# Retention attention and a gated MLP on one core: a new fixed order for all five engine queues

## The chip, the cores and the metric

The kernel runs on one core of one Trainium2 chip. The metric is device time in microseconds (us), from the start of an execution to its end; a result is the median of several runs. The kernel before takes 211.69 us, the median of 3 runs that lie between 211.59 and 213.75 us.

A core has five engines with a queue of instructions each, worked off in order: TensorE (PE, matmuls and transposes), VectorE (DVE), ScalarE (ACT), GpSimd (POOL) and SyncE (SP), which here issues the DMA transfers of the main work. An engine waits with all that stands behind an instruction until the data of that instruction are there. So the order in which instructions are put into each queue is itself a part of the kernel, and it is the part that changes here.

## The reference

```python
# q, k, v: (8 batches, 8 heads, 576, 64)
scores = (1 / sqrt(64)) * q @ k^T                  # per batch and head
D[i, j] = gamma[h] ** (i - j) if i >= j else 0
x = (scores * D) @ v                               # no softmax
x = x.transpose(0, 2, 1, 3).reshape(8, 576, 512)
h = gelu_tanh(x @ w_in)                            # w_in: 512 x 1024
u, v = h[..., :512], h[..., 512:]
v_n = layernorm(v) * g_ln                          # over the 512
v_s = einsum('ts,bsd->btd', w_sg, v_n) + b_sg      # w_sg: 576 x 576, mixes positions
out = x + (u * v_s) @ w_out                        # w_out: 512 x 512, float32 out
```

The attention has no softmax, only a decay with the distance. So it can be done in chunks: inside a chunk the masked scores, and from one chunk to the next a running sum of k^T v per head (called Z here). The second half is a gated MLP whose gate mixes the 576 positions of a batch through `w_sg`.

## The kernel before

**Tiling.** The 8 batches go in 4 pairs (p = 0 to 3). A pair has 1152 rows, 9 tiles of 128; tile 4 lies half in one batch and half in the other. For the attention each pair is cut into 5 units (two tiles, two tiles, the middle tile, two tiles, two tiles), so there are 20 units, 0 to 19; units 2, 7, 12 and 17 are the middle ones, of half the width. Tiles are numbered 0 to 35 through all pairs.

**The jobs.** The program is built as 925 jobs, numbered in the order in which `add` is called. A job is a few instructions on one engine. Those that the text speaks of, with the lines of their instructions in the kernel before:

- loads on SP, 512 KB each in most cases (`a_load`, L457 and L460; the middle units take the L460 line, two transfers of 128 KB), `load(b,q)`, `load(b,k)` and `load(b,v)` of unit b. For most units one load of q of 1 MB serves two units.
- casts to bfloat16, with the decay factors multiplied in for q and v (`a_prep`: L493 k, L503 q and v), on POOL; unit 0 has its q on DVE and its k on ACT (L491).
- `T`: transposes of q and k on PE (`a_T`, L540), taken to SBUF by DVE (L555). From unit 10 on, all but the middle units have theirs transposed by DMA instead (`a_TX`, L560).
- `S`: scores (`a_S`, L591), masked on DVE (L604). `Z`: the running sum (`a_Z`, L627), added up on DVE and cast on ACT. `O` and `O2`: the attention's output in two parts (`a_O`, `a_O2`, L673), brought to x by ACT (L730).
- `V` (`m_V`, L741) and `U` (`m_U`, L788): x times the two halves of w_in. After V come gelu on ACT (L748), statistics on DVE (L756, L757), the rs group, one over the standard deviation, on POOL (L761 to L764), and the norm on ACT (L773 for the middle tile, L776 for others). After U comes gelu on ACT (L798).
- `W`: the spatial mixing of a batch (`m_W`, L807), multiplied with u on DVE (L817). It needs the norms of all five tiles of its batch and the transposed spatial weight.
- `m_O(i)`: the output of tile i (L838). For the first pair x is added by further matmuls (L833) and the result evacuated on ACT (L853); later pairs have x transposed back by a DMA (`m_X`, L847) and added on DVE (L855). Then a store on SP (`m_store`, L860).

**The start.** The weights come in through the same SP queue: the second half of w_in (for V), w_sg in three pieces (two large ones of 576 KB and a small one), the first half of w_in (for U) and w_out. ACT and DVE cast w_in (L388, L390), ACT casts w_sg (L413). Then ten jobs on PE transpose the spatial weight (`build_wT`, L921), each with an evacuation on DVE. `to_col`, `to_rows`, `place_vmid` and `place_wT` (L909 to L914) put g_ln and b_sg into additional rows of the operands of W. `fill(n)` (L357) puts matmuls on zeros into PE's queue, whose result nobody reads, n units of 128 columns.

**What sets the order.** A string `ORDER` lists all job numbers, and a name such as `f10` for `fill(10)`. In the kernel before, `plan` calls `follow`: it takes from `ORDER` only the order within each engine, estimates each job's start with a small cost model (semaphores, DMA rings, blocks of instructions, changes of kind on PE), and `emit` writes the jobs in the order of these estimated starts. Per engine this is again the order of `ORDER`. The order between engines does matter for which buffers are shared: a tile pool hands its buffers out in rotation, in the order of the calls. The numbers of buffers are fixed in `BUFS`: 8 for loads (`ld`), 2 for the large q (`ldq`), 2 each for the casts of q and k and for the transposed q and k, 2 PSUM buffers for T, S and O (`pp`), 4 for everything else in PSUM (`d`), 3 for V's gelu (`vg`), 4 for the output (`ob`), 5 for x transposed back (`xr`).

## Time and profile before

| | |
|---|---|
| median of 3 runs (lowest to highest) | 211.69 us (211.59 to 213.75) |
| profiled execution, span from first to last instruction | 211.8 us |
| PE busy (matmuls) | 193.5 us, 91% |
| PE's weight loads, beside the matmuls | 134.4 us, 63% |
| DVE busy | 146.7 us, 69% |
| ACT busy | 116.3 us, 55% |
| POOL busy | 117.9 us, 56% |
| HBM read and written | 32.79 MB and 9.44 MB, 199 GB/s |

The span is the time between the first and the last instruction of one profiled execution, and it is within 0.1 us of the median. A busy share is the share of that span. In the lists of waits and of the chain, an arrow `<-` names what ended the wait: a job on another engine by its line, a DMA by its tensors, or "issue", where nothing that the profile shows was waited for. In names such as `qb<-ld,gpow` the output stands on the left and the inputs on the right.

### The profile page before, as it was taken

What the parts mean: (1) busy time and instruction counts of PE and PEld (TensorE: products, weight loads), DVE (VectorE), ACT (ScalarE), POOL (GpSimd) and SP (SyncE); (2) the same over time, 40 slices, a digit from 0 to 9 for tenths busy, and PEclk for the clock granted to TensorE, in tenths of its full rate; (3) what the DMA queues carried; (4) which work ended last, traced back from release to release, by engine and by line L of the source; (5) the groups of instructions that cost most, each with busy time, mean ns of one, the idle gap of its engine ahead of it and who ended that gap; (6) DMA issues with size and microseconds to landing.
All of it is one profiled execution on the core that took longest, in us unless ns stands there. A gap on an engine that the chain in (4) does not pass through costs nothing.

```text
span 211.8 us, 7654 instructions
## 1 busy us (share of the span) xinstructions
PE 193.5 (91%) x3257; PEld 134.4 (63%) x3288; DVE 146.7 (69%) x287; ACT 116.3 (55%) x207; POOL 117.9 (56%) x169
## 2 busy tenths in 40 slices
PE   7995598799999999989999979989989999999992
PEld 6873366576677666757676657656647676565660
DVE  4585487978767688648767647778676757977483
ACT  5233656993696753784775745617544574363400
POOL 8738375897599699920849598044349440322000
PEclk9999889999999999999999999999999999999999
DMA  5999899999799999999898989999789986936685
GB/s 157 334 274 323 140 377 273 259 347 320 146 316 319 317 208 289 181 258 326 245 253 110 219 155 345 237 129 248 197 217 264 254 193 187 225 115 149 176 249 198
DMA packets 94228, 50.45 MB, mean 238 GB/s; under 512 B 45354, under 2 KB 87602, under 8 KB 94194
## 3 DMA queue, kind: packets, MB, share of 16 engines
q1 hardware_dynamic: 94176, 49.97, 96.9%
q8 instruction: 25, 0.41, 0.9%
q14 instruction: 9, 0.07, 0.2%
q10 hardware_dynamic: 18, 0.00, 0.0%
HBM read 32.79 MB, written 9.44 MB: 199 GB/s over the span
## 4 chain that ended last, share of the span: by engine, by line
PE 62%; DMA 16%; SPq 5%; POOL 5%; DVE 3%; ACT 3%; issue 3%; POOLq 0%; ACTq 0%
PE wp L807 15%; PE op L838 11%; PE hu L788 11%; PE hv L741 11%; PE pp L673 5%; DMA xT<-in_moe_w_sg_dram 4%; DMA xT<-in_moe_w_in_dram 4%; PE pp L591 3%; DMA ld<-in_k_dram 3%; DMA kT<-kb 3%; SPq L560 3%; DMA ld<-in_q_dram 2%; PE zp L627 2%; SPq L457 2%; POOL vb L503 2%
## 5 line engine op out<-in xcount | busy, mean ns | idle before, releaser
L604 DVE TENSOR_TENSOR ret<-pp,msk 128x1024 bf16<-128x1024 f32 x32 | 38.7, 1216 | 6.4 <-PE pp L591 6.4
L503 POOL TENSOR_TENSOR vb<-ld,gpow 128x1024 bf16<-128x1024 f32 (+1 forms) x20 | 34.6, 1731 | 14.7 <-DMA ld<-in_v_dram 9.1
L807 PE MATMUL wp<-wT,vn 128*128 128x288 bf16 x256 | 40.8, 286 | 0.0
L788 PE MATMUL hu<-xT,w_in 128*128 128x256 bf16 (+1 forms) x320 | 36.7, 262 | 0.2 <-ACT zb L659 0.2
L741 PE MATMUL hv<-w_in,xT 128*128 128x512 bf16 x125 | 35.1, 380 | 1.4 <-issue 0.3
L817 DVE TENSOR_TENSOR uT<-wp,uT 128x288 bf16<-128x288 f32 x64 | 27.9, 449 | 11.5 <-PE wp L807 11.0
L838 PE MATMUL op<-w_out,uT 128*128 128x512 bf16 (+1 forms) x136 | 34.3, 373 | 0.6
L730 ACT ACTIVATE xT<-pp 128x512 bf16<-128x512 f32 (+1 forms) x40 | 20.6, 552 | 25.8 <-PE pp L673 24.0
L788 PEld LDWEIGHTS <-w_in 128*128 128x128 bf16 x320 | 28.2, 98 | 7.0 <-issue 0.5
L756 DVE BATCH_NORM_STATS2 bst<-vg 128x6 f32<-128x512 f32 x36 | 24.7, 687 | 10.1 <-ACT vg L748 10.0
L776 ACT ACTIVATE vn<-vg,mv 128x512 bf16<-128x512 f32 x32 | 25.3, 807 | 11.1 <-POOL mv L764 11.0
L748 ACT ACTIVATE vg<-hv 128x512 f32<-128x512 f32 x36 | 21.3, 594 | 17.0 <-PE hv L741 13.3
L807 PEld LDWEIGHTS <-vn 128*128 128x128 bf16 x256 | 24.2, 98 | 8.4 <-issue 0.2
L761 POOL TENSOR_SCALAR mv<-mv 128x2 f32<-128x2 f32 (+1 forms) x20 | 4.5, 224 | 42.2 <-DVE mv L757 38.3
L503 POOL TENSOR_TENSOR qb<-ldq,gpow 128x1024 bf16<-128x1024 f32 x14 | 26.5, 1902 | 0.9 <-DMA ldq<-in_q_dram 0.8
L798 ACT ACTIVATE uT<-hu 128x512 bf16<-128x512 f32 x36 | 20.9, 595 | 7.9 <-PE hu L788 7.9
L855 DVE TENSOR_TENSOR ob<-op,xr 128x512 f32<-128x512 f32 (+1 forms) x28 | 18.4, 668 | 6.1 <-PE op L838 5.8
L838 PEld LDWEIGHTS <-uT 128*128 128x128 bf16 x148 | 13.7, 98 | 11.5
L741 PEld LDWEIGHTS <-xT 128*128 128x128 bf16 x144 | 13.2, 98 | 11.6 <-ACT xT L730 0.2
L807 PE MATMUL wp<-wT,vmid 128*128 128x288 bf16 x64 | 18.3, 287 | 0.0
L493 POOL CAST kb<-ld 128x1024 bf16<-128x1024 f32 x14 | 14.4, 1038 | 4.3 <-DMA ld<-in_k_dram 4.2
L762 POOL TENSOR_TENSOR mv<-mv,mhalf 128x2 f32<-128x2 f32 (+1 forms) x20 | 13.7, 686 | 1.7
(100 smaller groups left out, 248.9 us busy)
## 6 DMA issues: line engine op xcount, KB each, us to landing
out_dram<-ob SPq DMA_DIRECT2D x35, 256.0 KB, 3.5
ld<-in_k_dram SPq DMA_DIRECT2D x16, 512.0 KB, 6.9
ld<-in_v_dram SPq DMA_DIRECT2D x16, 512.0 KB, 6.7
ldq<-in_q_dram SPq DMA_DIRECT2D x7, 1024.0 KB, 8.4
xT<-in_moe_w_sg_dram SPq DMA_DIRECT2D x2, 576.0 KB, 9.0
ld<-in_q_dram SPq DMA_DIRECT2D x2, 512.0 KB, 6.3
xT<-in_moe_w_in_dram SPq DMA_DIRECT2D x1, 1024.0 KB
ld<-in_q_dram SPq DMA_DIRECT2D x8, 128.0 KB, 5.9
```

The source lines that it names most:

```text
L503: ve.tensor_tensor(dst, src, g.unsqueeze(len(src.shape) - 1).to_broadcast(list(src.shape)), op=Alu.mult)
L604: ins = nc.vector.tensor_tensor(ret[:].rearrange("p r (k t) -> p (r k) t", k=2), sc[:].rearrange("p r (k t) -> p (r k) t", k=2), (msk2 if ...
L730: nc.scalar.activation(dst, src, Act.Copy)
L741: ins = nc.tensor.matmul(hv[:], xTs[p][:, m, kk, :], w_in[:, kk, F2:], start=(kk == 0), stop=(kk == KK - 1))
L748: unfence(nc.scalar.activation(vgs[i][:], cur.pop(("hv", i))[:], Act.Gelu_apprx_tanh), ("V", i))
L756: nc.vector.bn_stats(bst[:], vgs[i][:])
L776: nc.scalar.activation(vn[:], vg[:], Act.Identity, scale=mv[:, s, 2:3], bias=mv[:, s, 3:4])
L788: ins = nc.tensor.matmul(hu[:, n, :], w_in[:, kk, 128 * c:128 * c + 128], xTs[p][:, m:m + w, kk, :], start=(kk == 0), stop=(kk == KK - 1), ...
L798: unfence(nc.scalar.activation(uTs[p][:, c0:c1, 128 * m:128 * m + 128 * w], cur.pop(("hu", i, half))[:], Act.Gelu_apprx_tanh), ("U", i, half))
L807: ins = nc.tensor.matmul(ps[:], vns[t0 + j][e][:, 128 * c:128 * c + 128], wT[e][j][:, half * HS:(half + 1) * HS], start=(j == 0), stop=(j ...
L817: ins = nc.vector.tensor_tensor(uTs[p][:, c, col:col + HS], cur.pop(("wp", b, c, half))[:], uTs[p][:, c, col:col + HS], op=Alu.mult)
L838: ins = nc.tensor.matmul(op[:], uTs[p][:, c, r], w_out[:, c, cs], start=(p >= XP and c == 0), stop=(c == KK - 1), skip_group_check=True)
```

## The change

Jobs, buffers and their numbers stay. The string `ORDER` is replaced by another one, which orders the same 925 jobs anew on all five queues, and `plan` takes the jobs straight from it: they are emitted in the order of the string, engines mixed as they stand there. The cost model (`ready`, `place`, `follow`, the tables at the top) is taken out; `ins` of some jobs changes, which nothing reads any more. The filler has two entries, `f1` and `f5`, in place of eight, 6 units instead of 47.

```diff
-SEM = {"PE": 205.0, "DVE": 35.0, "ACT": 35.0, "POOL": 35.0}
-OVL = {"PE": 0.0, "DVE": 60.0, "ACT": 90.0, "POOL": 50.0, "SP": 0.0}
-FETCH = (5400.0, 5000.0)
...
 ORDER = (
-    '0 f1 1 f3 2 f3 f2 72 f10 3 73 17 f5 103 6 104 7 106 105 75 107 f9 8 76 5 195 267 197 268 f14 269 4 22 198 16 15 '
-    '108 196 12 13 272 109 79 273 14 74 111 274 276 275 110 112 277 270 199 80 20 201 278 289 23 279 202 19 21 9 290 '
...
+    '2 f1 0 1 7 74 6 105 f5 75 3 103 76 12 104 267 106 8 269 107 17 195 108 197 77 198 196 109 72 14 73 111 268 272 '
+    '112 5 13 273 274 78 199 4 79 275 15 201 276 16 202 110 23 9 277 81 278 113 24 270 200 279 114 115 80 280 22 '
...
     def plan(self):
-        if ORDER:
-            return self.follow(ORDER)
...
+        self.done = [self.fill(int(x[1:])) if x[0] == "f" else self.jobs[int(x)] for x in ORDER.split()]
 
     def emit(self):
+        seen = set()
         for j in self.done:
+            assert all(d in seen for d in j.deps)
+            seen.add(j)
             j.fn()
+        assert all(j in seen for j in self.jobs)
```

The start of SP's queue, in the words of the list above (win1 is the half of w_in for V, win0 that for U, sg the large pieces of the spatial weight, sg4 its small piece):

```
before: q0 k0 v0 win1 sg4 q1 k1 v1 sg  sg q2 k2 v2 q3 win0 k3 k4 v3 k6 v4 k5 ...
after:  v0 q0 k0 k1 q1 win1 q2 v1 sg4 v2 k2 sg sg q3 win0 k3 k4 v3 v5 v4 k5 ...
```

And somewhat later, from the 27th entry on (st is a store of an output tile):

```
before: ... k7 v7 v8 q8 k8 k10 st1 q10 k9 k11 v9 q12 k12 v10 st2 st3 v11 st0 ...
after:  ... v6 q8 k8 k9 st2 st1 v7 v8 q10 v10 k10 k11 v9 st0 st3 x9 q10T k10T st4 ...
```

On PE the first jobs are, without the filler (wT is a build, with batch parity and column block; U has tile, width and half; W has batch, block and half):

```
before: T(0) col S(0,0) Z(0) S(0,1) O(0) rows1 O2(0) T(1) V(0) S(1,0) S(1,1) Z(1) V(1) wT(0,2) wT(0,0)
        O(1) T(2) O2(1) wT(1,4) rows0 wT(1,0) S(2) V(2) O(2) wT(0,1) wT(0,3) wT(1,2) Z(2) O2(2) V(3) ...
after:  col Z(0) T(0) S(0,0) S(0,1) rows0 T(1) O(0) O2(0) S(1,0) rows1 S(1,1) V(0) V(1) Z(1) T(2) Z(2)
        S(2) O(1) O2(1) O(2) O2(2) wT(0,1) wT(0,4) wT(1,1) wT(1,0) wT(1,2) V(2) wT(0,0) wT(1,4) V(4) ...
```

## The prediction

> **What bounds the kernel now.** I read the busy totals and the slices of the page first, then a table of stages, and then who TensorE (PE) waited for.

> ```profile
> span 211.8 us, 7654 instructions
> ...
> PE 193.5 (91%) x3257; PEld 134.4 (63%) x3288; DVE 146.7 (69%) x287; ACT 116.3 (55%) x207; POOL 117.9 (56%) x169
> ...
> q8 instruction: 25, 0.41, 0.9%
> ```
> ```profile
> 0.00:46.00 46.00, 37.21 (x712) 28.71 (x716) 30.62 (x73) 26.19 (x44) 30.46 (x57) 0.96 1.00 272
> 46.00:205.00 159.00, 153.25 (x2536) 104.18 (x2556) 113.36 (x210) 90.08 (x164) 87.46 (x114) 1.00 0.99 229
> ```
> ```profile
> 0.00:16.00 16.00, 12.54 (x52) 10.47 (x52) 1.00 0.98 255
> ```

> The columns are the stretch, its length, busy time and count of PE, weight loads, DVE, ACT and POOL, then the granted clock, the DMA share and GB/s. The third fence is the same table for line L357 alone, the filler. The first W job, the spatial mixing, starts at 46 us. Before it PE does only 37.2 - 12.5 = 24.7 us of real work in 46; after it, it is busy 153.25 of 159 and idle 5.75. So there are two places to win or lose: how much real work is done by 46 us, and the idle time after it. The waits of PE after 46 us:

> ```profile
> PE pp L673 <- issue: 1.2, 2, 0.9
> PE pp L591 <- DMA kT<-kb: 1.0, 1, 1.0
> PE pp L540 <- POOL qb L493: 1.0, 1, 1.0
> ```

> Three kinds of wait hold 3.2 of the 5.75 us. No large stall waits to be removed: the change can lift these and can make others of the same kind.

> **The change, part by part.** No job, buffer or byte changes except the filler. The planner's code leaves the host's side; it costs the chip nothing either way. What is left is positions in five in-order queues.

> *The start.* These rows tell when each load was there, by the first work that uses it:

> ```profile
> 5.19 1.23 DVE L503 TENSOR_TENSOR qb<-ld,gpow 128x1024 bf16<-128x1024 f32 x1 [0.84 <-DMA ld<-in_q_dram]
> ...
> 6.94 1.06 ACT L491 ACTIVATE qb<-ld 128x1024 bf16<-128x1024 f32 x1 [1.51 <-DMA ld<-in_k_dram]
> ...
> 8.87 1.90 POOL L503 TENSOR_TENSOR vb<-ld,gpow 128x1024 bf16<-128x1024 f32 x1 [1.33 <-DMA ld<-in_v_dram]
> ...
> 12.14 1.06 ACT L390 ACTIVATE w_in<-xT 128x1024 bf16<-128x1024 f32 x1 [4.14 <-DMA xT<-in_moe_w_in_dram]
> ...
> 14.40 1.90 POOL L503 TENSOR_TENSOR qb<-ld,gpow 128x1024 bf16<-128x1024 f32 x1 [3.63 <-DMA ld<-in_q_dram]
> ...
> 23.22 1.83 ACT L413 ACTIVATE wnat<-xT 128x576 bf16<-128x576 f32 x3 [1.73 <-DMA xT<-in_moe_w_sg_dram]
> ...
> 26.42 1.05 POOL L503 TENSOR_TENSOR vb<-ld,gpow 128x512 bf16<-128x512 f32 x1 [0.49 <-DMA ld<-in_v_dram]
> ...
> 35.14 0.64 PE L540 MATMUL pp<-ident,qb 64*128 64x64 bf16 x32
> ...
> 37.99 1.04 POOL L493 CAST kb<-ld 128x1024 bf16<-128x1024 f32 x1 [0.65 <-DMA ld<-in_k_dram]
> ...
> 44.21 1.65 ACT L773 ACTIVATE vmid<-vg,mv 64x512 bf16<-64x512 f32 x2 [0.18 <-POOL mv L764]
> ...
> 46.01 0.66 PE L807 MATMUL wp<-wT,vn 128*128 128x288 bf16 x4
> ```

> A 512 KB load takes 1.8 us of the queue (5.19, 6.94, 8.87). In the new order v, q and k of unit 0 arrive at about 5.2, 6.9 and 8.8, so the first transposes, which wait for both casts, start near 10. k and q of unit 1 come next, near 10.3 and 11.9 instead of 14.4; the first half of w_in slips by two such loads, 12.1 to about 15.5. The q of unit 2, v of unit 1, the small piece of the spatial weight and v and k of unit 2 now also stand ahead of the spatial weight's two large pieces. The first fifteen transfers are the same set in both orders, so what follows them (k of units 3 and 4, there at 37.99) is as early as before; the spatial weight takes the place in which unit 2's v landed, 26.4 instead of 23.2. Its casts, which ended at 25.05, then end near 28.5, and the builds start there.

> What PE does meanwhile is gained: S, Z and O of units 1 and 2, four of which stood behind the builds, come first. Walking the list with durations of before, T of unit 3's q is reached near 37 (35.14 before, where two of the ten builds came after it; now one does). Then the k of units 3 and 4 decides: T of k cannot run before 37.99 + 1.04, and the new POOL order puts one rs group (1.4) ahead of these casts, so 40.4 at the earliest; its evacuation (1.2), S, an S that waits for the other's evacuation, and W near 44.4 to 45.7. ACT's `place_vmid` (2.5 us) no longer stands in front of the norms that end at 45.9. Against 46.0 that is 0.3 to 1.6 sooner, but the O of unit 3 comes after W now, so 0.7 us less work is done by then. I take **-0.2**, with -2 and +2 as ends: the sooner end is a W that waits for nothing but the 40.4, the later one the 3.2 us of the spatial weight with two thirds uncovered.

> *The filler.* 47 units become 6. They take 12.5 us in which PE waits for loads, so removing them saves nothing by itself. What they may cover is the clock:

> ```profile
> 21.00:25.00 4.00, 1.36 (x35) 0.64 (x35) 2.34 (x3) 2.27 (x5) 0.82 (x2) 0.99 0.84 130
> 25.00:28.40 3.40, 3.29 (x75) 2.67 (x75) 1.97 (x6) 1.14 (x4) 1.97 (x3) 0.50 0.92 277
> ```

> After 4 us with 1.36 busy, the granted clock is 0.50 for 3.4 us, which costs 1.7 us of PE's time in before as well. I count one such stretch in each kernel, at 0. [...]

> *Changes of kind on PE.* Jobs are of three kinds (wide matmuls, attention, transposes). A change costs about a tenth of a microsecond:

> ```profile
> 73.74 0.57 PE pp L540 x32
> ...
> 77.04 0.25 PE zp L627 x28
> ...
> 92.12 1.73 PE hv L741 x8
> 93.84 0.87 PE hu L788 x8
> 94.72 0.61 PE wp L807 x5
> ...
> 98.81 0.57 PE pp L591 x32
> 99.38 0.72 PE wp L807 x5
> ```

> The rows are a T, a Z, two V, a U, a W, two S and a W. The second W stands at such a change, the first does not: 0.11. From the first W on there are 67 changes instead of 70: **-0.3**. The others that go are in the start, where PE waits anyway.

> *Blocks of instructions.* 25 fetches bring 0.41 MB, 16.4 KB each, for 3257 + 3288 = 6545 recorded PE instructions: about 256 in a block. One wait shows what a short block does:

> ```profile
> 85.27 0.23 PE pp L591 x14
> ...
> 89.39 0.26 PE pp L591 x16
> 89.65 0.05 PE pp L673 x3
> 89.69 0.94 issue
> 90.63 0.30 PE pp L673 x5
> ```

> PE stops in the middle of one job, with nothing to wait for but its instructions. Counting matmul and load as two, the 256 before the stop began at the piece of 85.27 and held 4.4 us of work; with the 0.94 the block took 5.3. I take 5.3 us as the least time of a block. In the new order I count off the blocks, with the durations of before and 0.1 for each change. One example: W, S and T of units 7 and 8, U, V, O of unit 7, Z and half an S of unit 8 make 256 instructions and 0.61 + 0.28 + 0.57 + 0.87 + 0.87 + 0.2 (20 of the small matmuls) + 0.25 + 0.15 and five changes, 4.3 us at most. Four blocks after the first W fall short: 4.3, 4.9, 4.2 (with 0.15 for the narrow S in the example) and 4.6, so 1.0 + 0.4 + 1.1 + 0.7 = 3.2 us of waiting. Before paid 1.2 (the "issue" row above). **+2.0**; ends -1.2 (all hidden) and +3.

> *Loads behind stores.* In before, SP issues `load(7,v)` (job 40) ahead of the store of output tile 1 (job 345); now it stands behind the stores of tiles 2 and 1.

> ```profile
> 55.67 0.89 SPq L460 DMA_DIRECT2D ld<-in_v_dram  x1
> ```
> ```profile
> 60.07 0.60 ACT L853 ACTIVATE ob<-op 128x512 f32<-128x512 f32 x1 [0.44 <-PE op L838]
> ```
> ```profile
> 69.57 0.68 PE pp L673 x40
> ```
> ```profile
> 150.43 0.57 SPq L860 DMA_DIRECT2D out_dram<-ob  x1
> ```
> ```profile
> ld<-in_k_dram SPq DMA_DIRECT2D x8, 128.0 KB, 5.6
> ld<-in_v_dram SPq DMA_DIRECT2D x8, 128.0 KB, 4.2
> ```

> Before, this load left at 55.7, some 14 us ahead of Z of unit 7 (just after the 69.57 row). Now the chain begins with matmul `m_O(1)`: two evacuations of unit 5, a norm and its own evacuation on ACT (0.6 + 0.6 + 0.8 + 0.6, the 0.8 worked out from 1.65 for the middle tile's two, ending 2.6 after its start), a store's issue 0.6, two load issues 1.1 (as long as the store's), landing 4.2, POOL's half-width multiply 1.05 (the 26.42 row): 9.55 us. PE has 8.05 us of work between, plus changes 0.5 and a block's 0.4: 8.9. **+0.6**; all of PE's queue stands behind that Z. Ends: 0, and 3.6 with the landing of the k row (+1.4), both issues as slow as the 0.89 of the 55.67 row (+0.7) and ACT one evacuation and one norm later (+1.0). Behind it are the O of output tile 0 and a U, none of which can pass.

> The DMA-transposed units, where 1.0 was waited (kT), lie as far behind their POOL casts in PE's work as before, some up to 3 us less (unit 10), some up to 2 us more (unit 13): 0, with 1.0 either way. `T` of unit 17, where another 1.0 was waited (qb), keeps its place behind its loads: 0.

> *Sum.* 211.8 - 0.2 - 0.3 + 2.0 + 0.6 = 213.9. The median of 211.69 lies 0.1 below the profiled span, so I say **213.9** as a measured time to be read loosely in its last digit, 1.0% slower. A measurement of this kernel tells about 1% from no change, which is 209.6 to 213.8.

> **Rivals.**
> 1. *It ends sooner.* The blocks are fetched early enough (before ran all but one or two of its blocks without a wait), W comes at 43.9 with nothing lost (-1.4), and half of the 5.75 us of idle time goes with the rearranged loads (-2.3): 211.8 - 0.3 - 1.4 - 2.3 = 207.8. For it: the units 0 to 2 are done before the builds, and the transposed units 13 and 15 get their loads earlier. Against: the three waits have three different causes, and the distances were short in both orders.
> 2. *The store gate decides.* If the chain to unit 7's Z runs at its slow end, 3.6 instead of 0.6: 216.9. It decides from a chain of 8.9 us. For it: the chain has six links on four queues, and each can only be late; against: 4.2 us is the median of eight such loads.
> 3. *The clock.* PE stays at half clock from its first job on and pays a second stretch of 1.7 us on the path, as S and O of unit 0 and both V run twice as long: 215.6. For it, the two rows on the clock; against, these jobs wait for loads.
> 4. *The blocks are hidden and the rest cancels*: 213.9 - 2.0 = 211.9. [...] The 0.94 us row shows one that was not.

> **How the numbers follow.** Forecast (212 to 216) 0.45, of it 0.18 within 1%; rival 1 0.30, of it 0.03 within 1%; rival 2 0.12; rival 3 0.06; rival 4 0.07. Faster 0.27, same 0.28, slower 0.27 + 0.12 + 0.06 = 0.45. The range reaches to rival 1 and to rival 2 with a little beyond: 207 to 217.5. Alone, the forecast would have 212 to 216.

> **What would show it.** The first W between 44 and 46.5 with the builds starting after 28; "issue" waits in the middle of a job three to five times after 46 us, 3 us in all; an idle PE before Z of unit 7, with SP's load directly behind the store. If "issue" stays near 1.2 the block term was wrong; if W starts near 43 or after 48, the start was. A clock row of 0.5 twice would speak for rival 3.

## The result, and the profile after

The changed kernel takes 220.63 us (median of five runs, 218.22 to 221.15), the kernel before 213.55 (five runs, 211.59 to 214.67): 1.036 times as long, with an interval of 1.029 to 1.044. On another occasion the same pair gave 1.029 (1.018 to 1.041). It is slower, as forecast, but by more than three times the forecast 1.0%, and 220.63 lies above the range of 207 to 217.5. All ratios here leave out the executions that took over 1.5% longer than the fastest of the same kernel.

A run's time is 1.7 us more than its span in most of these runs (218.22 against 216.5). By this difference the span of 211.8 from which the prediction started belongs to a time of about 213.5, not to the median of 211.69 beside which it was put.

The totals of the page after, then who PE waited for after 46 us (the wait in all, how often, the longest):

```profile
span 216.5 us, 7572 instructions
...
PE 190.8 (88%) x3216; PEld 130.9 (60%) x3244; DVE 149.7 (69%) x287; ACT 116.5 (54%) x207; POOL 118.6 (55%) x169
```
```profile
PE pp L404 <- POOL qb L357: 2.3, 1, 2.3
PE zp L491 <- POOL vb L367: 1.7, 2, 1.1
PE wp L671 <- issue: 0.7, 1, 0.7
...
PE pp L455 <- issue: 0.3, 1, 0.3
PE op L702 <- issue: 0.2, 1, 0.2
```

PE is busy for 2.7 us less than before. The filler takes 9.6 us less (2.9 instead of 12.5), and the rest of PE's work 6.9 us more, part of it at half clock: the granted clock is 0.50 from 7.8 to 24.8 us, from 28.2 to 35.1 and from 158.0 to 161.4. The span is 4.7 us longer. The largest wait is T of unit 17 (2.3). The waits with "issue", in which the blocks of instructions were to be seen, come to 1.2 in this trace, about as much as before.

To see where the 4.7 us arise, take for each job on PE its start on the clock less the work of all PE jobs ahead of it in its own list, with one fixed duration for each kind (W 0.61, U and V 0.87, S 0.26, T 0.565, O with O2 0.69, an output 0.865 and so on). The result is what PE has lost to waits, changes and clock by then. Other durations would shift the rows, but nearly alike, so read the differences between rows:

```
work done, us        24     60     96    120    126    end
before             24.3   26.3   30.0   32.5   33.8   35.3
changed            25.7   28.7   31.4   33.6   37.8   40.0
changed, 2nd trace 25.1   28.4   29.9   32.6   36.9   39.6
```

At the first W (24) the changed kernel is about 0.8 to 1.4 us behind, and at 96 it is level or 1.4 behind. Between 120 and 126, where T of unit 17 stands, it loses 4.2 or 4.3 us where the kernel before loses 1.3: 3 us more. Both traces are of the fastest of their executions (218.22 and 217.85 us); what the others lost beyond that has no trace.

**Two holes in the loads.** The queue of SP in the first 24 us (its waits, and rows in order of time: start, length), then from 53 to 71 us:

```profile
SPq L266 <- DVE w_in L252: 3.3, 1, 3.3
```
```profile
18.86 2.05 DVE L252 CAST w_in<-xT 128x1024 bf16<-128x1024 f32 x1
...
20.94 1.88 SPq L266 DMA_DIRECT2D xT<-in_moe_w_sg_dram  x2
```
```profile
54.66 3.90 SPq L321 DMA_DIRECT2D ld<-in_k_dram  x2
65.38 4.23 SPq L724 DMA_DIRECT2D out_dram<-ob  x2
69.70 1.31 SPq L324 DMA_DIRECT2D ld<-in_v_dram  x2
```
```profile
SPq L724 <- ACT ob L717: 10.2, 2, 6.7
```

The two large pieces of the spatial weight land in the buffer of w_in's half, so SP has to wait until DVE has cast that half, and the cast now stands behind two masks, memsets and evacuations on DVE: 3.3 us in which no load is issued. And from 58.6 to 69.2 SP waits 10.2 us for the output tiles of two stores, with all the loads behind it. The stages around it, after and then before (the last two columns are the DMA share and GB/s):

```profile
58.00:64.00 6.00, 5.89 (x98) 3.92 (x99) 5.48 (x10) 5.43 (x10) 4.24 (x6) 1.00 0.98 269
64.00:70.00 6.00, 5.95 (x134) 3.79 (x133) 3.77 (x6) 5.38 (x11) 3.67 (x6) 1.00 0.14 50
```
```profile
64.00:70.00 6.00, 5.95 (x104) 4.22 (x107) 3.89 (x6) 4.03 (x9) 5.54 (x8) 1.00 1.14 330
```

PE itself notices nothing there (5.95 of 6 busy in both). But for 6 us little is loaded (50 GB/s), where the kernel before moves 330 GB/s.

**The wait at T of unit 17.** The chain that leads to it (start, length), and POOL behind it:

```profile
151.93 0.63 SPq L324
...
152.60 3.91 DMA ld<-in_k_dram
...
156.64 0.62 POOL qb L357
...
157.31 0.41 PE pp L404 x16
```
```profile
156.64 0.61 POOL L357 CAST qb<-ld 128x512 bf16<-128x512 f32 x1 [4.59 <-DMA ld<-in_k_dram]
160.31 1.90 POOL L367 TENSOR_TENSOR qb<-ldq,gpow 128x1024 bf16<-128x1024 f32 x1 [3.06 <-DMA ldq<-in_q_dram]
162.17 1.05 POOL L367 TENSOR_TENSOR vb<-ld,gpow 128x512 bf16<-128x512 f32 x1
```

The k of unit 17 leaves SP at 151.9 (149.0 before), while T of unit 17 stands 3.2 us of work earlier on PE than before. Behind the cast POOL waits another 3.1 us for the q of unit 18, a load of 1 MB that left SP at 126 before and leaves it at 153.3 now; v of unit 17, for O of unit 17, stands behind that on POOL. That the hole at 64 us is what makes this load late is a theory so far; the experiments test it.

### The profile page after: what moved, and what is told of

Same layout as the page of the kernel before. It is cut to its first block, busy times and chain, and to the rows that moved or that the text cites. A ratio compares the mean times of both kernels' runs of the same rounds, so it can differ in the third digit from the quotient of the medians.

```text
span 216.5 us, 7572 instructions
## 1 busy us (share of the span) xinstructions
PE 190.8 (88%) x3216; PEld 130.9 (60%) x3244; DVE 149.7 (69%) x287; ACT 116.5 (54%) x207; POOL 118.6 (55%) x169
## 4 chain that ended last, share of the span: by engine, by line
PE 63%; DMA 10%; POOL 9%; ACT 4%; issue 4%; DVE 4%; SPq 4%; POOLq 0%; ACTq 0%
PE wp L671 15%; PE hu L652 12%; PE hv L605 11%; PE op L702 10%; PE pp L537 5%; DMA ld<-in_v_dram 5%; PE pp L455 4%; POOL vb L367 3%; DMA ld<-in_q_dram 3%; POOL qb L367 3%; PE wtp L785 2%; PE pp L404 2%; SPq L321 2%; DMA ld<-in_k_dram 2%; DVE ret L468 2%
## 5 line engine op out<-in xcount | busy, mean ns | idle before, releaser
L671 PE MATMUL wp<-wT,vn 128*128 128x288 bf16 x256 | 41.4, 289 | 1.2 <-issue 0.7
L605 PE MATMUL hv<-w_in,xT 128*128 128x512 bf16 x129 | 37.7, 402 | 1.1 <-issue 0.4
L652 PE MATMUL hu<-xT,w_in 128*128 128x256 bf16 (+1 forms) x320 | 36.2, 262 | 0.1
L652 PEld LDWEIGHTS <-w_in 128*128 128x128 bf16 x320 | 28.2, 98 | 6.6 <-ACT w_in L254 0.2
L620 DVE BATCH_NORM_STATS2 bst<-vg 128x6 f32<-128x512 f32 x36 | 24.7, 685 | 8.0 <-ACT vg L612 7.9
L367 POOL TENSOR_TENSOR qb<-ldq,gpow 128x1024 bf16<-128x1024 f32 x14 | 26.4, 1902 | 6.3 <-DMA ldq<-in_q_dram 6.3
L625 POOL TENSOR_SCALAR mv<-mv 128x2 f32<-128x2 f32 (+1 forms) x20 | 4.8, 241 | 41.5 <-DVE mv L621 37.2
L605 PEld LDWEIGHTS <-xT 128*128 128x128 bf16 x144 | 14.0, 102 | 14.2 <-issue 2.6
L357 POOL CAST kb<-ld 128x1024 bf16<-128x1024 f32 x14 | 14.2, 1039 | 1.0 <-DVE run L516 1.0
## 6 DMA issues: line engine op xcount, KB each, us to landing
ld<-in_q_dram SPq DMA_DIRECT2D x8, 128.0 KB, 7.4
```

Of the source, the lines that this page charges most:

```text
L367: ve.tensor_tensor(dst, src, g.unsqueeze(len(src.shape) - 1).to_broadcast(list(src.shape)), op=Alu.mult)
L605: ins = nc.tensor.matmul(hv[:], xTs[p][:, m, kk, :], w_in[:, kk, F2:], start=(kk == 0), stop=(kk == KK - 1))
L620: nc.vector.bn_stats(bst[:], vgs[i][:])
L652: ins = nc.tensor.matmul(hu[:, n, :], w_in[:, kk, 128 * c:128 * c + 128], xTs[p][:, m:m + w, kk, :], start=(kk == 0), stop=(kk == KK - 1), ...
L671: ins = nc.tensor.matmul(ps[:], vns[t0 + j][e][:, 128 * c:128 * c + 128], wT[e][j][:, half * HS:(half + 1) * HS], start=(j == 0), stop=(j ...
```

## The experiments

Most edits are moves within the order of one or two queues; entries of a queue are shown in its order. a_warm2, b_nofill and a_fill17 change the filler, and the crosses further down join two orders. The kernels that follow the order of before are written with the changed kernel's code, so their lines are numbered as there.

**Again, the second stretch of half clock, one load, and the filler of before.**

```diff
 a_again: the changed kernel, unchanged
 a_warm2, in S of unit 2, ahead of its matmuls:
+            for _ in range(6):
+                nc.tensor.matmul(sc[:, 0, :256], warm[:, :128], warm[:, :256], ...)
 a_k17, SP:
-load(17,q) X(14) store(10) X(16) store(11) X(17) X(15) store(12) load(17,k)
+load(17,q) load(17,k) X(14) store(10) X(16) store(11) X(17) X(15) store(12)
 b_nofill, PE of the kernel before:
-f1 f3 f3 f2 f10 f5 T(0) ... f9 ... f14 ...
+f1 f5 T(0) ...
```

> The changed kernel once more, unchanged, for a second trace beside the first and on the same chip as the next three. Every theory expects the same 1.036 (1.029 to 1.044) times the kernel before. In the trace: the granted clock at 0.50 in two stretches before the first W (about 8 to 25 us and 28 to 34 us in the first trace) and once after T of unit 17 (near 160 us), the wait of T of unit 17 near 2.3 us, and the first W near 47 us.

> The changed kernel with six matmuls on zeros (about 1.5 us at full clock) ahead of S of unit 2, in the PSUM tile which that S then overwrites; PE waits there for 1.54 us anyway, and is at 0.50 for 5.7 us from 28.3 us on. Theory clock: the half clock in this stretch is what makes the start late, since PE is busy there without a gap up to the first W; with it gone, the stretch of 5.7 us loses 2.8 us, the first W comes at 44 to 45 instead of 46.9, and the time falls by 2 to 2.8 us. Rival loads: the casts of the spatial weight and the k of units 3 and 4 set the first W; the clock is full, but W stays within 0.7 us of 46.9 and the time within 1 us.

> The changed kernel with one load moved on SP: k of unit 17 stands right behind q of unit 17, ahead of four transposes of x by DMA and three stores; in the changed kernel it leaves SP at 151.9 us and its cast ends at 157.3, when PE has waited 2.25 us at T of unit 17 and then runs 3.4 us at clock 0.50. Theory queue: the wait falls to 0.3 us or less and the 0.50 stretch near 160 us is gone, so 2.0 + 1.7 = 3.5 to 4 us less. Rival: another operand is as late (q of unit 17, or the transposes of x and the stores that are now later), a wait of 1 to 2 us shows up within 10 us behind, and the time falls by less than 1.5 us.

> The kernel before in its own order, with the eight entries of filler cut to the two that the changed kernel has (1 and 5 units). Nothing else differs. Theory clock: without filler PE falls to 0.50 within the first 12 us and stays there for 10 us or more; S, O and V of units 0 and 1 run twice as long, the builds begin about 1 us later, and the time is 1 to 3 us more. Rival: PE waits for loads in this stretch whatever its clock, so the time is within 1 us of before, or less, since the filler itself no longer stands in front of O of unit 0.

Measured against before: a_again 1.029 (1.018 to 1.041), a_warm2 1.028 (1.017 to 1.039), a_k17 1.028 (1.021 to 1.036), b_nofill 1.004 (0.998 to 1.010).

Clock: without filler PE does run at half clock. The page's clock does not say so in this run (1.00 throughout, its first record is at 20 us), but the transposes of T do (min, median, max in ns): without filler they take what they take in the changed kernel at a granted clock of 0.50 (the second fence), and in before, at 1.00, they take less (the third):

```profile
L404 PE MATMUL pp<-ident,qb x64: 230/238/238, 7.9 to 18.4; 64*128 64x64 bf16 x64
```
```profile
L404 PE MATMUL pp<-ident,qb x64: 231/238/238, 10.3 to 16.1; 64*128 64x64 bf16 x64
```
```profile
L540 PE MATMUL pp<-ident,qb x64: 190/190/200, 8.2 to 17.8; 64*128 64x64 bf16 x64
```

And it costs nothing that can be measured: PE waits for loads there. In a_warm2 the stretch of 0.50 near 28 us is gone, the first W comes at 45.5 instead of 46.3 (a_again) or 46.9, which lies between the two expectations, and the time does not fall; the six matmuls became twelve and took 2.86 us, 1.3 more than the wait. So the half clock near 28 us makes the first W late, but it is not the cause of the longer time.

The move of one load takes the wait at T of unit 17 from 2.3 to 0.45 us and the half clock behind it away, and the time stays: in its place PE waits for x of unit 15 (1.2; the transposes of x, which free x's buffer, are now later), for two v of POOL's (1.2), for an output tile (0.8) and for v of unit 17 (0.6). The trace also has 1.2 us of "issue" in a T at 57 us, which a_again has not. The rival holds: the wait moved.

**Crosses of the two orders.** Four kernels take the first part of one order and then what is left in the other's.

```diff
 h_bW_a : kernel before up to its first W, then the changed order
 h_aW_b : changed kernel up to its first W, then the order before
 h_b96_a: kernel before up to 96 us of PE's work, then the changed order
 h_a96_b: changed kernel up to 96 us of PE's work, then the order before
```

> A cross of the two orders: the kernel before up to its first W (177 entries of its order, with its filler), then all that is left in the order of the changed kernel. Measured so far, PE's clock time less the work done: the changed kernel is 0.7 to 1.4 us behind at the first W, 0 to 1.3 us behind when 96 us of PE's work are done, and 4.3 to 4.7 us behind at the end. Theory tail (the loss is made behind 96 us of work, by the order there): 3 to 4.5 us slower than before. Theory start (the hole of 3.3 us that SP's wait for the cast of w_in leaves in the loads is carried along until the slack is used up): within 1 us of before.

> The other way round: the changed kernel up to its first W (164 entries), then all that is left in the order of before. Theory tail: 0.5 to 1.5 us slower than before, which is what the start itself loses. Theory start: 3 to 4.5 us slower than before.

> The kernel before until 96 us of PE's work are done (568 entries, about 125 us on the clock), then what is left in the order of the changed kernel. Theory tail: 3 to 4 us slower than before, with a wait of 1 us or more at T of unit 17 or in its place. Theory start: within 1 us of before.

> The changed kernel until 96 us of PE's work are done (557 entries), then what is left in the order of before. Theory tail: 0 to 1.5 us slower than before. Theory start: 3 us slower or more, since the loads of the last two pairs come through the same late queue.

Measured: 1.024 (1.006 to 1.043), 1.019 (1.006 to 1.032), 1.022 (1.004 to 1.040), 1.026 (1.007 to 1.045). By the times none of the theories comes out, since all four are alike. The loss count says more for the first two: from the first W to the end h_bW_a loses 14.3 us and the changed kernel 14.3 and 14.6, h_aW_b loses 10.0 and before 11.0. So the part behind the first W costs 3.3 us or more in the changed order, with either start. What h_aW_b loses, it loses ahead of its first W, which comes at 51.0, later than in either kernel, so its seam has a price of its own.

One thing in h_bW_a speaks against a fixed path from the hole to unit 17. SP stands for 10.5 us at the same two stores, and the DMA share from 64 to 70 us is 0.28. Yet the k of unit 17 leaves SP at 148.7, T of unit 17 waits only 0.5 us, and no half clock follows. The same order behind the first W loses as much there, at other places, four Z among them (2.8 us). The two cuts at 96 lose 4 to 5 us at the seam itself, within 6 us of work, and tell nothing.

**Unit 17 and the cast of w_in.**

```diff
 a_fill17, PE:        V(27) +f7 T(17) V(28) S(16,1) ...
 a_T17late, PE (and T's evacuation on DVE to match):
-V(27) T(17) V(28) S(16,1) S(17) W(5,2,0) m_O(14) W(5,3,1) U(27,2,0) U(27,2,1)
+V(27) V(28) S(16,1) W(5,2,0) m_O(14) T(17) W(5,3,1) U(27,2,0) S(17) U(27,2,1)
 a_cast, DVE:         the cast of w_in (L252) from behind the evacuation L755
                      to ahead of zero_wnat (L758), four jobs earlier
 a_cast_T17:          both of the last two
```

> The changed kernel with seven units of filler (about 1.9 us) ahead of T of unit 17 on PE, where PE waited 2.25 to 2.4 us in both traces and ran at clock 0.50 for 3.4 us from some 3 us later on. Nothing comes earlier by it. Theory double price (the stall costs its own length and then 1.7 us of half clock): the stall as seen before T stays within 0.5 us, the 0.50 stretch near 160 us is gone, V of unit 28 takes 0.87 instead of 1.6 us, and the time falls by 1.7 us against the changed kernel. Rival: the half clock was covered by other waits; the time stays within 0.5 us, with waits behind T of unit 17 that sum to over 1 us.

> The changed kernel with T of unit 17 four jobs later on PE (behind V of 28, S of 16, a W and the output of tile 14, 2.7 us of work), its evacuation and S of unit 17 later to match; the load that it waits for stays where it is. Theory distance (PE reaches T 3 us of work earlier than in the order before, while its load leaves SP 3 us later): the stall falls from 2.25 to under 0.5 us, no half clock follows, and 3 to 4 us are gone from the time. Rival: the next operands on the same queues (v of unit 17 and 18, x of unit 15) are as late, as after the earlier load of k in the run before; other waits take 2 us or more of it back, and the time falls by less than 1.5 us.

> The changed kernel with one DVE instruction moved: the cast of half of w_in stands ahead of the zeroing of the spatial weight's margins, five jobs earlier, at 16.2 instead of 18.9 us. In the changed kernel the two large pieces of the spatial weight leave SP only at 20.9, when this cast has read their buffer; SP stands still for 3.3 us and the loads behind it with it. Theory hole: SP issues them at 17.6, the casts of the spatial weight end some 3 us sooner (30.0 before), the builds start at 29 or sooner instead of 31.2, the first W comes 1 us sooner or more, and the time falls by about 1 us. Rival: the chain of x of unit 0, V, gelu, place_vmid, T of unit 2 sets the start; the builds start where they did within 0.5 us, and the time stays within 0.5 us.

> Both moves, the early cast and the later T of unit 17. By the theories hole and distance 4 to 5 us less than the changed kernel, which is within 1 us of before; by the rivals 0 to 2 us less.

Measured: a_fill17 1.024 (1.014 to 1.033), a_T17late 1.030 (1.013 to 1.046), a_cast 1.019 (1.007 to 1.031), a_cast_T17 1.020 (1.002 to 1.037).

The stretch behind T of unit 17, in the changed kernel and with the filler ahead of T (granted clock, DMA share, GB/s at the end):

```profile
157.60:160.90 3.30, 3.30 (x48) 1.67 (x41) 0.69 (x1) 1.08 (x2) 0.59 (x1) 0.55 1.09 333
```
```profile
155.70:159.00 3.30, 3.30 (x62) 1.95 (x63) 1.43 (x3) 1.09 (x2) 0.07 (x1) 1.00 1.07 342
```

With filler in the wait the clock stays, and V of tile 28 ("unit 28" in the expectation) takes 1.0 us as elsewhere. The stall does have a second price. In the trace 2.8 us are lost between 120 and 126 us of work instead of 4.2 and 4.3, but 5.0 instead of 2.2 and 2.7 behind that, with waits of 1.0 in a W and 1.2 at Z of unit 19, and the span is 216.1 as in a_again: the rival. The times differ by less than their intervals; how much stays is open.

With T of unit 17 later, nothing waits at T, and PE waits for v of unit 17 instead:

```profile
PE pp L537 <- POOL vb L367: 1.9, 1, 1.9
```

In POOL's queue that v stands behind the q of unit 18, whose load left SP at 155.4. Rival again. This trace also has 3.8 us of "issue" (1.2 in the changed kernel), of which 3.2 are at two places before 60 us, far from the edit; so the run says little about the move itself.

The early cast lets the first large piece of the spatial weight leave SP at 17.7 and shortens SP's first hole from 3.3 to 1.9 us. (The trace now puts that wait down to a DVE instruction that stands behind the cast; what it is for is open.) But the spatial weight is cast no sooner, in the changed kernel and then with the early cast:

```profile
SPq L266 <- DVE row4b L755: 1.9, 1, 1.9
```
```profile
26.50 0.67 ACT L277 ACTIVATE wnat<-ld 64x576 bf16<-64x576 f32 x1
```
```profile
26.55 0.67 ACT L277 ACTIVATE wnat<-ld 64x576 bf16<-64x576 f32 x1
```

The builds begin at 31.0 instead of 31.2. On ACT these casts follow place_vmid and a gelu of V without a wait, so it is ACT's queue that sets them, and the rival put down for this run holds: the first hole does not delay the builds. The first W does come at 45.5, and what was lost by then is 24.3 us as in before. What goes with that is the half clock: the stretch near 28 us lasts 3.4 us here instead of 6.8. In the four runs with the changed start in which it lasts 3.4 us or is absent (a_warm2, a_cast, a_store_cast, h_a96_b, of which two have no early cast) the first W comes at 45.5 to 45.6; in the eight with 6.8 us, a_cast_T17 with its early cast among them, at 46.2 to 47.1. (h_aW_b is left out, for its seam.) The wait of 2.1 at T of unit 17 stays, and 1.019 is not told from the changed kernel by its interval.

a_cast_T17 is at 1.020, where the theories had put it within 1 us of before: its first W comes at 47.1, and O of unit 17 waits 3.1 us for its v, with half clock behind it.

**The holes.** a_store takes the two stores away from the front of the loads; a_store_cast adds the early cast; b_gate puts one store in front of loads in the kernel before.

```diff
 a_store, SP:
-load(9,k) store(2) store(1) load(7,v) load(8,v) load(10,q) load(10,v) load(10,k) load(11,k)
+load(9,k) load(7,v) load(8,v) load(10,q) store(2) load(10,v) load(10,k) store(1) load(11,k)
 b_gate, SP of the kernel before:
-load(7,k) load(7,v) load(8,v) load(8,q) load(8,k) load(10,k) store(1) load(10,q)
+load(7,k) store(1) load(7,v) load(8,v) load(8,q) load(8,k) load(10,k) load(10,q)
```

> The changed kernel with two stores moved on SP: those of output tiles 2 and 1 stand behind three and five of the loads that they stood ahead of (v of units 7 and 8, q, v and k of unit 10), as loads stood ahead of stores in the order before. In the changed kernel SP waited 6.7 and 3.5 us for these stores' data, from 58.6 to 69.2 us, and from 64 to 70 us the DMA engines were busy 0.14 of the time (1.14 in before). Theory gate: this hole is what makes the later loads late; with it gone, k of unit 17 leaves SP before 150 instead of at 151.9, the stall at T of unit 17 is under 0.7 us, no half clock follows, and the time falls by 3 us or more. Rival tight order: the loads of units 11 to 17 wait for buffers and for POOL, not for the queue; SP is as late as before at 100 us, T of unit 17 still waits 2 us or its loss moves to its neighbours, and the time falls by less than 1 us.

> The same with the cast of w_in five jobs earlier on DVE as well, which has taken away SP's first hole (3.3 us at 17.6 us). Theory gate with theory hole: the two holes together make the whole loss, the time is within 1 us of before, or less. Rival tight order: not more than 2 us less than the changed kernel.

> The kernel before with one store moved on SP: that of output tile 1 stands five loads earlier, ahead of v of units 7 and 8, q and k of unit 8 and k of unit 10. Its data are there near 60.7 us, SP reaches it at 54.7, so SP stands for about 6 us and issues nothing. Z of unit 7 needs the load behind it at 70 us, so there it costs nothing. Theory gate: the hole in the loads comes out later, at the transposed units or at T of unit 17, and the time is 1.5 to 4 us more than before. Rival: the slack of the order before (loads lie some 10 us ahead) takes it up, the time is within 1 us of before.

Measured: a_store 1.012 (1.005 to 1.019; 215.73 us), a_store_cast 1.022 (1.015 to 1.029), b_gate 1.029 (1.024 to 1.035).

In a_store the stage without loads is gone, and PE's waits behind 96 us are small:

```profile
64.00:70.00 6.00, 5.95 (x148) 3.93 (x147) 3.38 (x6) 5.38 (x11) 4.07 (x7) 1.00 1.05 264
```
```profile
PE wp L671 <- DVE ob L719: 1.2, 1, 1.2
PE zp L491 <- POOL vb L367: 0.5, 1, 0.5
PE pp L404 <- POOL qb L357: 0.5, 1, 0.5
```

The k of unit 17 leaves SP at 147.7, T waits 0.5, no half clock follows. At 126 us of work 31.6 us are lost, 2.2 less than in before and 6.2 less than in the changed kernel; at the end 36.0, against 35.3 and 40.0. All that theory gate put down for this run was met.

b_gate is the counterpart. One store in the wrong place costs the kernel before 2.9%. Its stages, SP and POOL:

```profile
52.00:58.00 6.00, 5.70 (x135) 4.26 (x133) 4.86 (x10) 4.34 (x9) 3.34 (x6) 1.00 0.49 88
58.00:64.00 6.00, 5.95 (x121) 3.78 (x120) 3.89 (x7) 5.32 (x10) 1.71 (x1) 1.00 0.44 113
```
```profile
51.86 1.25 SPq L324 DMA_DIRECT2D ld<-in_k_dram  x1
59.60 0.37 SPq L724 DMA_DIRECT2D out_dram<-ob  x1
60.06 1.32 SPq L324 DMA_DIRECT2D ld<-in_v_dram  x2
```
```profile
65.02 1.05 POOL L367 TENSOR_TENSOR vb<-ld,gpow 128x512 bf16<-128x512 f32 x1 [5.31 <-DMA ld<-in_v_dram]
66.02 1.04 POOL L367 TENSOR_TENSOR qb<-ld,gpow 128x512 bf16<-128x512 f32 x1
67.02 1.90 POOL L367 TENSOR_TENSOR vb<-ld,gpow 128x1024 bf16<-128x1024 f32 x1
68.87 0.61 POOL L357 CAST qb<-ld 128x512 bf16<-128x512 f32 x1
```
```profile
PE pp L404 <- POOL qb L357: 3.2, 1, 3.2
PE wp L671 <- ACT vn L640: 1.7, 2, 0.9
```

SP stands 6.4 us, and the price falls where I had not looked: at T of unit 7, whose q and k had left SP before the hole. Their casts stand in POOL's queue behind the v of unit 7 that the hole delays (POOL waits 5.3 us for it), so the last of them ends at 69.5 and T waits 3.2. The hole is handed on by a second in-order queue.

a_store_cast missed. It should have been the best of the three. The stage without loads is gone there too (a DMA share of 1.04 from 64 to 70 us), and still it is at 1.022, no better than a_cast, which has the hole (1.019). That is what the rival "tight order" says: not more than 2 us less than the changed kernel. Its trace has T of unit 17 waiting 2.2 us and O of unit 17 1.8, with k leaving SP at 150.4 instead of 147.7, and 3.0 us of "issue" where a_store has 1.1. SP reaches the two stores sooner there and waits 5.0 us for them instead of 3.2, since their tiles come at the same time; which of these is the reason isn't shown.

**What is left.** The last runs put before's start ahead of the new order without the second hole, and move unit 17's loads.

```diff
 h_bW_store: kernel before up to its first W, then the order of a_store
 h_bW_store17 and a_store_17, SP:
-X(14) store(10) X(16) store(11) X(17) X(15) store(12) load(17,k) load(18,q) store(13) load(17,v)
+X(14) store(10) X(16) load(17,k) X(17) X(15) load(17,v) store(11) store(12) load(18,q) store(13)
```

> Both holes away in another manner: the kernel before up to its first W, then the changed kernel's order with its two stores behind the loads, as in the run that took the second hole away. From the parts measured: the start of before is 0.7 to 1.4 us better than that of the changed kernel, and behind the first W the changed order without the hole lost 10.7 us to waits and changes where before lost 11.0. Theory gate (the holes are the loss, the rest of the new order is as good as the old): 1 us slower to 1.5 us faster than before. Rival tight order: 2 us slower or more.

> The same, with the loads of k and v of unit 17 further ahead on SP as well (before two transposes of x, and before the 1 MB load of q of unit 18), at the cost of two stores. If supply at T and O of unit 17 is what is left of the loss (waits of 0.5 and 0.4 us in the run without the hole, 2.2 and 1.8 us in the one with the early cast), 0.5 to 1.5 us less than its twin. If a slot in the queue given to one load is taken from another, the same time within 0.5 us.

> The changed kernel's own start, its two stores behind the loads, and the loads of k and v of unit 17 ahead as in its twin. The same alternatives: 0.5 to 1.5 us less than without the move of unit 17 (1.012 times before), or the same within 0.5 us.

Measured: h_bW_store 1.013 (1.007 to 1.018), a_store_17 1.017 (1.008 to 1.026); h_bW_store17 is spread too widely for a ratio (220.7 us, 214.67 to 222.58). No kernel beats before. For h_bW_store, 1.013 is 2.7 us: the rival's "2 us slower or more" and not the theory's 1 us at most. It is level with before or ahead of it until 72 us of work (26.7 lost, 27.8 in before) and then loses 4.8 us within 6 us of work, at a place of its own, which the last section shows. The moves for unit 17 brought nothing. They put the q of unit 18 one load further back, v of unit 17 stands behind it on POOL, and O of unit 17 waits 3.8 and 4.0 us in their traces. Those traces are of executions of 220.9 and 224.6 us, among the longest of their kernels; whether the shorter ones wait there isn't shown.

So for the changed kernel as it stands, the two stores ahead of loads are the main cause: without the second hole the changed kernel is at 1.012 instead of 1.029 to 1.036, and a hole of its kind alone makes 1.029 out of the order before. Three things remain open. With the early cast the same move of the two stores gains nothing (1.022 and 1.019). With the start of before it gives 1.013 instead of 1.024, intervals that overlap. And T of unit 17 is only one of the places where the price can fall. The rest, about 1.2%, is partly the start (0.8 to 1.4 us, which go with the second stretch of half clock) and is not settled further.

## Why the prediction was wrong

**The sign and the place in the code were right, the price was read at the wrong job.** The step that failed is "Loads behind stores". It named the stores, their late tiles and the load behind them, and worked out what this does to Z of unit 7: +0.6. In the trace that load leaves SP at 69.7 and is there just in time: Z of unit 7 runs at 75.4 without a wait, the low end of the term. But the working stopped at this first load and put the rest of the queue at nothing. Behind `load(7,v)` stood v of unit 8, q, v and k of unit 10 and all that follows. SP stood 10.2 us, the DMA share fell to 0.14 (1.14 in before), and with the two stores behind these loads 1.7 to 2.4% of the time are gone, the wait at T of unit 17 with them (2.3 to 0.5). Rival 2 ("the store gate decides", 0.12, 216.9) was the right mechanism with the same wrong place.

**T of unit 17** was put at 0, since it "keeps its place behind its loads". It does on SP, with 80 entries ahead in both orders, but it stands 3.2 us of work earlier on PE, SP reached that entry 2.9 us later, and q of unit 18 moved from 126 to 153 us, ahead of unit 17's v on POOL. Measured: 2.3 of waiting (1.0 in before) and 1.7 of half clock.

**The blocks**, +2.0, were not there in the changed kernel's trace: 1.2 us of "issue" waits against 1.2 (and 0.2 with V) in before, and 1.2 again in a_again. Of the four blocks called short, the one worked out as the example shows a stop of 0.3 in place of 1.1, the others none; the stop of 0.7, in a W at 52 us, is ahead of the first of them. The 256 to a block were an estimate, from 6545 recorded instructions in 25 fetches (262 each). So the 5.3 us, taken from one stop, are no least time of a block. Rival 4 was right in this trace. But the term is not fixed by the order: other runs with the same order on PE show from 0.8 (a_cast) to 3.0 us (a_store_cast).

**The start**, -0.2, cost 0.8 to 1.4, within the ends given. What failed is that the casts of the spatial weight "end near 28.5, and the builds start there": they end at 30.1, and the builds begin at 31.2. The pieces did leave SP late, at 20.9, because of the buffer that they share with w_in, but a_cast shows that this is not what holds the builds; ACT reaches these casts only behind place_vmid and a gelu. The other step that failed is "I count one such stretch in each kernel, at 0": the half clock near 28 us lasts 6.8 us instead of 3.4, and the late first W goes with it. One more item was missed. Unit 0's q took 2.72 us on DVE instead of 1.23, and the cast of w_in 2.05 instead of 0.69, each beside a multiply on POOL.

**The filler** at 0 was right within the interval: 1.004 (0.998 to 1.010) without it. Its cover for the clock is worth nothing that these times show. Rival 3 had its sign, a clock row of 0.50 twice, and its second stretch does make the first W late, but not its price: without that stretch a_warm2 is at 1.028. The changes of kind (-0.3) are too small to be seen in any run.

**The base.** 213.9 was set beside 211.69, though it started from a span. With the 1.7 us that lie around a span the same sum would have read 215.6.

## What to carry to other kernels

A store that waits for the end of a long chain should not stand ahead of loads in an in-order DMA queue: two such stores cost the changed kernel as it stands 1.7 to 2.4%, one cost the kernel before 2.9%. Ask of each such wait how long the queue stands, what the transfers do meanwhile, and which engine's queue hands the lateness on; the job right behind the first load is only the first to ask. A stage in which PE is busy for 5.95 of 6 us and the DMA share falls to 0.14 (0.44 in b_gate) can be a debt that comes due later: 3.2 us within 10 us in b_gate, and by the theory that a_store bears out 2.3 us some 90 us later in the changed kernel. And a single late operand was not the bound in the runs for unit 17: where one load or job at a tight place is moved, the next operand has to be looked at before the run. Last, an edit moves all that stands behind it in time, the stops for instructions (0.8 to 3.0 us with this order on PE) and the half clock (3.4 us behind T of unit 17, or none) too, so one run of an edit shows the edit and these together.

## What the runs showed of the hardware

```
trace         stall, us   idle share of the windows   clock after
changed         2.25      0.66                        0.50 for 3.4 us
a_again         2.43      0.71                        0.50 for 3.4 us
h_bW_store      2.46      0.72                        0.50 for 3.4 us
h_b96_a         1.68      0.73                        0.50 for 3.4 us
b_nofill        1.90      0.56                        1.00
a_store_cast    2.21      0.54, next at most 0.3       1.00
a_cast          2.06      0.43, next at most 0.3       1.00
b_gate          3.23      0.46, 0.51                  1.00
```

In before and the changed kernel, the windows at full clock that were followed by half clock were idle for 0.66 to 1.00 of their length, all others for 0.46 or less. Over all twenty traces, counting the windows at full clock behind the first record of each, none that was idle for 0.47 or less was followed by half clock, and all with 0.59 or more were; from 0.48 to 0.56 nine were and nine were not, so there the idle share as the traces give it does not tell which.

**The page's clock can miss half clock at the start.** In a_again, a_k17 and b_nofill among others the page gives a clock of 1.00 for the first 20 us. But the 32 transposes of the first T take 1.03 us in a_again and in a_k17, as in the changed kernel, whose page gives 0.50 there (0.64 in before), and one takes 238 ns in b_nofill, as in the changed kernel, instead of 190 in before. The mean clock of a run can't be compared between runs for this reason.

**A block of instructions can be late by 2.5 us.** In h_bW_store PE stops in a T two matmuls before its end:

```profile
102.20 0.38 PE L404 MATMUL pp<-ident,qb 64*128 64x64 bf16 x14
105.05 0.20 PE L404 MATMUL pp<-ident,qb 64*128 64x64 bf16 x2 [2.46 <-issue]
```

By the transfer records the fetch of the next block left at 102.64, after the stop at 102.58; the one before had left at 92.25. The stop and the half clock behind it are most of the 4.8 us that this run lost there. h_bW_store17 and h_bW_a have the same order on PE. The first stops at the same matmul for 2.2 us; the second, whose fetch left at 102.44, for only 0.4:

```profile
104.97 0.20 PE L404 MATMUL pp<-ident,qb 64*128 64x64 bf16 x2 [0.36 <-issue]
```

It came to this matmul 2.0 us later, so PE goes on at 105.0 in both: what h_bW_store had gained by then, it lost here. The changed order shows the same. Its stop in the W at 52 us stands at one matmul in all eleven runs that keep this order so far, and lasts 0.5 to 1.6 us; one in a T near 57 us lasts 1.2 us in a_k17 and 1.8 in a_T17late, and is absent in a_again. So the order decides where PE can stop, and not for how long. From the fetch to the matmul with which PE goes on it is 2.4 us in h_bW_store (102.64 to 105.05), 2.5 in h_bW_a (102.44 to 104.97), 2.4 at the prediction's stop of 0.94 in before (88.20 to 90.63) and 2.6 at the stop in the W at 52 us in the changed kernel (50.06 to 52.64). What sets the time of the fetch wasn't found.
